# Wide DMA transposes, odd K heads through GpSimd's queue, and x kept by tiles, in a statically ordered two-layer attention and feed-forward kernel

## The chip, the cores and the metric

One core of one Trainium2 chip. The metric is device time in microseconds (us), lower is better. The six executions of the kernel before agree within 0.3%. Each run also lists the mean clock that TensorE was granted, as a share of full speed; it was between 0.97 and 1.00. The engines are TensorE (PE for its matmuls, PEld for its weight loads), VectorE (DVE), ScalarE (ACT), GpSimd (POOL) and the sync engine (SP), which here only issues DMAs.

## The reference

The input x has 2048 tokens of 512 values in bf16. Two times in turn: a memory-augmented attention, then a gated feed-forward layer, each on a layer-normalised x and with a residual sum.

```python
def reference(A_x, ...):
    x = A_x
    x = x + _A_ref(_layernorm(x), wq, wk, wv, wo, beta)   # 32 heads of 16, 4 segments of 512 tokens
    x = x + _B_ref(_layernorm(x), w1, w3, w2)             # silu(x w1) * (x w3), then w2; width 1376
    ... both once more ...

# _A_ref, for each segment s of 512 tokens and each head:
    p = softmax(q k^T * scale + causal mask);  a_dot = p v
    a_mem = (phi(q) M) / (phi(q) z + 1e-6)     # M, z: what earlier segments left
    o = g * a_mem + (1 - g) * a_dot            # then o @ wo
    M += phi(k)^T v;  z += sum(phi(k))
```

## The kernel before

The program lists its operations with what each reads and writes. A scheduler inside it then fixes, before anything runs, the order of instructions on every engine and the semaphore waits. It has a model of durations, and two tables (PRIO and GATE) that shift single groups of operations; the tables look fitted by search. At run time each engine goes through its list in this order, and what stands behind a waiting instruction starts later too: in the profile before, TensorE stood up to 1.7 us ahead of the memory update.

There are eight passes: two layers of four segments. Logits use four strips of the tensor array at a time (the four matmuls of a set start within 10 ns of each other, the median for 256 columns in the trace before). K of the odd heads is moved to other partitions, into `km`. Where data must be turned (tokens to columns or back), a DMA transpose of 128 x 512 elements does it, issued by the sync engine; only the x of the first two attention passes is turned on TensorE.

```python
xn_r = ring("xn", 4, [P, D])          # normalised x, one tile of 128 tokens each
xs_r = ring("xs", 4, [P, 512])        # attention outputs out of PSUM
xg_r = ring("xg", 3, [P, LT, 2, P])   # the same, turned

# normalise a tile, then turn it: one DMA a tile
S.add([o_dve(512, False, 1.45)], lambda e, ...: e.tensor_scalar(
    xn_r[xn.slot][:], x_tok[:, tt, :], mean, rstd, op0=ALU.subtract, op1=ALU.mult), ..., name="norm")
dmaT(lambda e, ...: e.dma_start_transpose(dt_[dst.slot][:, :, i * 128:(i + 1) * 128], xn_r[xn.slot][:, :]), ..., name="xT")
# (first two attention passes: four transposes on TensorE, line 628, instead of the DMA)

# odd heads of K, from the third pass on: 4 copies of 64 KB on the sync queue
S.add([("sp", 450.0, 2200.0)], lambda e, r=r: e.dma_start(km_r[z.km.slot][r], k_r[z.k.slot][r]), dmaq="sp", ..., name="km")

# memory update: pk turned by four DMAs, then 32 matmuls of 136 columns (line 735)
for G in range(NCG):
    dmaT(lambda e, G=G: e.dma_start_transpose(pkt_r[kt.slot][:, G, :, :], pk_r[pkb.slot][:, G, :]), ..., name="pkT")

# causal mask on the diagonal blocks, on GpSimd, after exp on ScalarE
pool(lambda e, ...: e.affine_select(e_r[ebuf.slot][:, :, c:c + 128], ..., fill=0.0), 512, ..., name="mask")

# attention output: two PSUM banks, two copies out, two DMAs
for X, xs, es in XS:
    ev(lambda xs=xs: xs_r[xs.slot][:], lambda X=X: bank(X), 512, ..., name="evX")
    dmaT(lambda e, ...: e.dma_start_transpose(dst(), xs_r[xs.slot][:]), ..., name="XT")
```

In the views below, line numbers of the kernel before and (in brackets) of the changed one are: projections of q and k 676 (677), of v 671 (672), logits 844 (852), probabilities times values 895 (903), memory update 735 (738), output projection 963 (952), gate and up 994 (983), down 1022 (1011), transposes of x on TensorE 628 (628), normalisation 618 (618), mask 866 (874). Of the names, `xn` is normalised x, `xs` attention outputs out of PSUM (TensorE's output memory, `psall`), `xg` the same turned, `og` the outputs made ready for the last projection, `e` the exponentials, `pk` phi(k). `W` is a set of buffers that many share: `W<-xn` turns x, `W<-W` turns pk, `W<-og` turns the outputs for the last projection.

Of the kernel before, what the change touches and what calls it, by code (L numbers as in the profile page):

```python
# [8 lines left out]
P = 128  # L9
# [16 lines left out]
LAT = 100.0  # L26
LAT_SAME = 50.0
DMA_SLACK = 500.0
# [4 lines left out]
SLACK = {"pe": 60.0, "act": 90.0, "dve": 60.0, "pool": 0.0, "sp": 300.0}  # L33
LOOK = {"pe": 90.0, "act": 90.0, "dve": 10.0, "pool": 10.0, "sp": 40.0}
C_AGE = 1200.0
MARGIN = {"rd": 200.0}
# [331 lines left out]
def o_pe(ns):  # L368
# [7 lines left out]
    ("", 0): 20, ("bnst", 3): -2.3, ("bnst", 7): -0.15, ("dacc", 4): -4, ("evX", 0): 1000.2, ("evk", 1): 1400,  # L376
    ("evk", 5): 1005, ("evq", 0): 300, ("evq", 7): 1751.7, ("evv", 0): 99.8, ("g", 3): -20, ("g", 5): 301.3,
    ("gp", 4): 998, ("hm", 6): 84.9, ("k", 4): -0.35, ("k", 5): 20.3, ("k", 7): -250, ("km", 2): -0.3,
    ("km", 4): 1000, ("ldwk", 0): -1.3, ("mblk", 2): 300, ("mrec", 3): -300, ("ph", 6): -0.6, ("phmin", 0): -100,
    ("phmin", 2): 0.05, ("q", 1): -300, ("q", 2): 0.6, ("q", 3): -550.05, ("q", 4): -0.3, ("q", 6): -999.7,  # L380
    ("rd", 0): 300, ("rdg", 1): -1, ("t", 7): -20, ("tanh", 5): -0.75, ("u", 1): -500, ("u", 4): -2002, ("u", 6): 780,
    ("v", 5): -0.15,
}
GATE = {
    ("bnst", 2): -1, ("bnst", 3): 1, ("bnst", 6): 3, ("ph", 0): -22, ("phexp", 0): -15, ("v", 1): -30, ("v", 6): 8,
    ("v", 7): 6,
# [3 lines left out]
def build(nc, A_x, A_wq, A_wk, A_wv, A_wo, A_beta, B_w1, B_w3, B_w2, out):  # L390
# [25 lines left out]
    xn_r = ring("xn", 4, [P, D])  # L416
# [7 lines left out]
    xs_r = ring("xs", 4, [P, 512])  # L424
    xg_r = ring("xg", 3, [P, LT, 2, P])
# [47 lines left out]
    def dmaT(fn, q="sp", **k):  # L473
        return S.add([(q, 1290.0, 2500.0)], fn, dmaq=q, mode="T", **k)
# [31 lines left out]
    if WARM:  # L506
        dve(lambda e: e.memset(xs_r[0][:], 0.0), 200, writes=["warm"], prio=CP - 1)

        def spin(e, B=new("B")):
            for _ in range(2):  # L510
                o = e.matmul(bank(B), xs_r[0][:, 0:128], xs_r[0][:], start=True, stop=True)
            return o
        wb = spin.__defaults__[0]
        pools["xs"].prev[0] = [pe(spin, 2 * MM512 * (2 if i < 4 else 1), reads=["warm"], writes=[(wb, 0)], bufs=[wb], prio=1e4, name="warm")
                               for i in range(WARM)]
# [14 lines left out]
    HEAD = (("sp", "q"), ("act", "3"), ("sp", "2"), ("act", "k"))  # L530
# [66 lines left out]
    def layer_norm(s, name, prio, gates=(), fine=False, turn=False, part=(0, LT), dst=None):  # L597
# [17 lines left out]
        for i in tiles:  # L615
            tt = 4 * s + i
            xn = new("xn")
            S.add([o_dve(512, False, 1.45)], lambda e, i=i, tt=tt, xn=xn: e.tensor_scalar(  # L618
                xn_r[xn.slot][:], x_tok[:, tt, :], ln_r[st.slot][:, i, 6:7], ln_r[st.slot][:, i, 9:10],
                op0=ALU.subtract, op1=ALU.mult), reads=[("x", tt), (st, 3, i), (st, 1, i)], writes=[(xn, 0)],  # L620
                bufs=[st, xn], hold=[dst], prio=prio, name="norm")
            if turn:
                B = new("B")
                tb = lambda B=B: bank(B).bitcast(BF16)[:, 0:512].rearrange("p (g c) -> p g c", g=NCG)

                def flip(e, xn=xn, tb=tb):
                    for cg in range(NCG):
                        o = e.transpose(tb()[:, cg, :], xn_r[xn.slot][:, 128 * cg:128 * cg + 128], ident[:])
                    return o
                pe(flip, 4 * 62, reads=[(xn, 0), "ident"], writes=[(B, 0)], bufs=[B, xn], prio=-900, name="xt")  # L630
                ev(lambda i=i: dt_[dst.slot][:, :, i * 128:(i + 1) * 128], tb, 512, reads=[(B, 0)], writes=[(dst, i)],
                   bufs=[B, dst], prio=-900, name="evt")
                continue
            dmaT(lambda e, i=i, xn=xn: e.dma_start_transpose(dt_[dst.slot][:, :, i * 128:(i + 1) * 128], xn_r[xn.slot][:, :]),
                 reads=[(xn, 0)], writes=[(dst, i)], bufs=[xn, dst], prio=prio, name="xT")
# [14 lines left out]
    def project(s, g, X, first):  # L650
        z = Seg()
        z.q, z.k, z.km, z.va = new("W"), new("W"), new("km"), new("va")
        if first:
            jobs = []
            for hf in range(2):
                for A in (0, 2):
                    jobs += [("q", (A, A + 1), hf), ("k", (A, A + 1), hf)]
# [3 lines left out]
        for n, (kind, Gs, hf) in enumerate(jobs):  # L661
# [5 lines left out]
            for a, G in enumerate(Gs):  # L667
                for cg in range(NCG):
                    st, sp_ = cg == 0, cg == NCG - 1
                    if kind == "v":  # L670
                        fn = lambda e, cg=cg, G=G, B=B, st=st, sp_=sp_: e.matmul(  # L671
                            bank(B), xa_r[X.slot][:, cg, 128 * G:128 * G + 128], wv_sb[:, cg, :], start=st, stop=sp_)
                        rd = [(X, G)]
                    else:
                        w = wq_sb if kind == "q" else wk_sb
                        fn = lambda e, cg=cg, G=G, B=B, st=st, sp_=sp_, w=w, a=a, W=W, c0=c0: e.matmul(  # L676
                            bank(B)[:, W * a:W * a + W], w[:, cg, 128 * G:128 * G + 128], xa_r[X.slot][:, cg, c0:c0 + W],
# [20 lines left out]
            elif kind == "k" and Gs[0] == NCG - 1:  # L698
                for pg in range(4):
                    r = slice(32 * pg + 16, 32 * pg + 32)  # L700
                    S.add([("sp", 450.0, 2200.0)], lambda e, r=r: e.dma_start(km_r[z.km.slot][r], k_r[z.k.slot][r]), dmaq="sp",
                          mode="T", reads=[(z.k, a, h) for a in range(NCG) for h in range(2)], writes=[(z.km, pg, "p")],
# [18 lines left out]
    def memory_update(g, z, pkb):  # L721
        kt = new("W")
        for G in range(NCG):
            dmaT(lambda e, G=G: e.dma_start_transpose(pkt_r[kt.slot][:, G, :, :], pk_r[pkb.slot][:, G, :]),
                 reads=[(pkb, G // 2)], writes=[(kt, G)], bufs=[pkb, kt], prio=g + 0.1, name="pkT")
        mb = new("mb")
        for hf in range(2):
# [10 lines left out]
            pe(fn, 8 * 65, reads=[(kt, 2 * hf), (kt, 2 * hf + 1)] + [(z.va, i) for i in range(LT)], writes=[(B, 0)],  # L738
# [49 lines left out]
    def unit_list(part):  # L788
# [9 lines left out]
        else:  # L798
            for G in (0, 2):
                out.append(([(A, ee, t1 - 1) for A in (G, G + 1) for ee in range(2)], []))  # L800
# [12 lines left out]
    JOIN = True  # L813
    HP = -1e6
# [6 lines left out]
    def attention(s, g, z, oms, parts):  # L821
        z.ot = new("W")
        cnt = 0
        for pi, part in enumerate(parts):
# [4 lines left out]
            for ui, (blocks, done, N) in enumerate(todo):  # L829
# [3 lines left out]
                for pgs in groups:  # L833
# [14 lines left out]
                    u = pe(lg, N / 2.4 + 20, mode="R", reads=[(z.k, b[0], b[2] // 2) for b in blocks] +  # L848
# [30 lines left out]
    def attend(s, g, z, pr, part, G, ees, where, xg, gates):  # L879
        t0, t1 = part  # L880
        W = 128 * (t1 - t0)
        both = W == 512 and len(ees) == 2
        sets = [(ee,) for ee in ees] if both else [ees]
        XS = [(new("B"), new("xs"), es) for es in sets]
        keys = [(G, ee, j) for ee in ees for j in range(t1)]
        spot = {ee: (X, W * es.index(ee)) for X, xs, es in XS for ee in es}

        def av(e):
# [11 lines left out]
        pe(av, ncol / 2.4 + 10 * len(keys), mode="C", reads=[t for k in keys for t in where[k][3]] + [(z.va, j) for j in range(t1)],  # L900
           writes=[(X, 0) for X, xs, es in XS], bufs=[X for X, xs, es in XS] + [z.va] + list(ebs.values()),
           hold=[xs for X, xs, es in XS], prio=pr, gates=gates, name="C%d.%d" % (G, ees[0]))
        for X, xs, es in XS:
            ev(lambda xs=xs: xs_r[xs.slot][:], lambda X=X: bank(X), 512, reads=[(X, 0)], writes=[(xs, 0)], bufs=[X, xs],
               prio=g - 100.2, name="evX")
            if len(es) == 1:
                dst = lambda es=es: xg_r[xg.slot][:, :, es[0], :]
            else:
                dst = lambda: xg_r[xg.slot][:].rearrange("p t e c -> p (t e) c")[:, 0:4, :]
            dmaT(lambda e, dst=dst, xs=xs: e.dma_start_transpose(dst(), xs_r[xs.slot][:]), reads=[(xs, 0)],  # L910
                 writes=[(xg, ee) for ee in es], bufs=[xs, xg], prio=pr, name="XT")

    def normalise(g, z, part, G, xg, oms):
# [8 lines left out]
        sums = lambda: xg_r[xg.slot][:].rearrange("p t e (a c) -> p (t e a) c", c=32)[:, 0:n, 16]  # L922
        gv = lambda: gg[:, 1, 8 * G:8 * G + 8].rearrange("p (a e) -> p e a", e=2)

        def scaled(e):
            a, b = rd_r[rd.slot][:, 0, 0:n], rd_r[rd.slot][:, 1, 0:n]
            if full:
                v = "p (t e a) -> p t e a"
                w = gv()[:, None, :, :].to_broadcast([P, nt, 2, 4])
            else:  # L930
                v = "p (e t a) -> p e t a"
                w = gv()[:, :, None, :].to_broadcast([P, 2, nt, 4])
            return e.tensor_tensor(b.rearrange(v, e=2, a=4), a.rearrange(v, e=2, a=4), w, ALU.mult)
        dve(lambda e: e.reciprocal(rd_r[rd.slot][:, 0, 0:n], sums()), 7.2 * n, reads=[(xg, 0), (xg, 1)], writes=[(rd, 0)],
            bufs=[xg, rd], prio=pr, name="rd")
        dve(scaled, n + 90, reads=[(rd, 0), "g1"], writes=[(rd, 1)], bufs=[rd], prio=pr, name="rdg")
        ogv = lambda: og_r[og.slot][:].rearrange("p t (a e d) -> p t a e d", e=2, d=DH)
        for k in range(2):
            def fn(e, k=k):
                if full:  # L940
                    src = xg_r[xg.slot][:, :, k, :].rearrange("p t (a c) -> p t a c", c=32)[:, :, :, 0:16]
                    r = rd_r[rd.slot][:, 1, 0:n].rearrange("p (t e a) -> p t e a", e=2, a=4)[:, :, k, :]
                    return e.tensor_tensor(ogv()[:, :, :, k, :], src, r[:, :, :, None].to_broadcast([P, nt, 4, DH]), ALU.mult)
                src = xg_r[xg.slot][:].rearrange("p t e c -> p (t e) c")[:, 2 * k:2 * k + 2, :]
                r = rd_r[rd.slot][:, 1, 4 * nt * k:4 * nt * k + 4 * nt].rearrange("p (t a) -> p t a", a=4)
                return e.tensor_tensor(ogv()[:, 0:nt, :, k, :], src.rearrange("p t (a c) -> p t a c", c=32)[:, :, :, 0:16],
# [163 lines left out]
```

## Time and profile before

| | before |
|---|---|
| time, median of 6 runs | 500.5 us (499.94 to 501.57) |
| span of the profiled run | 498.1 us |
| TensorE busy, idle by the profile | 480.9 us, 17.2 us |
| VectorE, ScalarE, GpSimd busy | 403.4, 394.3, 235.9 us |
| sync queue in DMA issues | 259 us |
| DMA transposes | 180 |

TensorE is busy all but 17 us. These are the issues that the change touches, with the median time from issue to landing in the last column:

```profile
km<-W SPq DMA_DIRECT2D x24, 64.0 KB, 2.4
...
xg<-xs SPq DMA_TRANSPOSE x64, 2.4
...
W<-xn SPq DMA_TRANSPOSE x56, 2.5
```

### The profile page before, as it was taken

The numbers are of one execution on the slowest core, as the hardware profiler recorded it, in microseconds if no ns is written. First come the engines' busy times: TensorE is split into PE (matmuls) and PEld (weight loads), VectorE is DVE, ScalarE is ACT, GpSimd is POOL, SyncE is SP. The second block draws the span as 40 slices with busy tenths as digits, with TensorE's granted clock in tenths as the row PEclk, the third lists the DMA queues.
The fourth block names the chain that finished last, engine by engine and source line by source line (L and its number), as shares of the span: only waits on it lengthen the run. The fifth ranks groups of instructions, "written<-read, shape, count | busy, mean of one in ns | idle before, by whom it ended". The sixth has DMA issues, their size and how long they took to land.

```text
span 498.1 us, 10481 instructions
## 1 busy us (share of the span) xinstructions
PE 480.9 (97%) x4198; PEld 214.9 (43%) x4198; DVE 403.4 (81%) x802; ACT 394.3 (79%) x350; POOL 235.9 (47%) x350
## 2 busy tenths in 40 slices
PE   7999898999999999999999999999999999999997
PEld 4443335654444344344444344444344334444443
DVE  5899998997888689889967889889984797479572
ACT  3999898899989997799988999788987898731230
POOL 4857444575455555645544436445645563610000
PEclk9999999999999999999999999999999999999999
DMA  6956834422232241341441303522322222220201
GB/s 198 313 89 128 137 74 96 67 59 48 54 68 52 64 70 38 76 86 22 68 93 43 75 22 75 95 45 54 71 49 54 53 43 54 65 53 12 74 1 42
DMA packets 104160, 35.86 MB, mean 72 GB/s; under 512 B 96976, under 2 KB 102096, under 8 KB 104112
## 3 DMA queue, kind: packets, MB, share of 16 engines
q1 hardware_dynamic: 102432, 31.94, 31.1%
q0 software_dynamic: 720, 2.46, 1.8%
q10 hardware_dynamic: 960, 0.79, 0.6%
q8 instruction: 33, 0.54, 0.5%
q14 instruction: 15, 0.12, 0.1%
HBM read 8.43 MB, written 2.10 MB: 21 GB/s over the span
## 4 chain that ended last, share of the span: by engine, by line
PE 74%; DVE 16%; DMA 4%; ACT 3%; issue 1%; SPq 1%; POOL 0%
PE psall L994 29%; PE psall L1022 15%; PE psall L844 8%; PE psall L676 7%; PE psall L895 5%; PE psall L963 3%; PE psall L671 3%; DVE ln L605 2%; ACT e L853 2%; DVE xn L618 2%; DVE W L481 2%; DVE x_tok L967 2%; DVE W L713 1%; DVE xs L481 1%; DMA W<-W 1%; DVE W L715 1%
## 5 line engine op out<-in xcount | busy, mean ns | idle before, releaser
L853 ACT ACTIVATE e<-psall 128x2048 bf16<-128x2048 f32 (+1 forms) x180 | 301.0, 1702 | 37.9 <-PE psall L844 36.0
L866 POOL TENSOR_SCALAR_AFFINE_SELECT e<-e 128x512 bf16<-128x512 bf16 x256 | 163.5, 658 | 165.4 <-ACT e L853 164.0
L994 PE MATMUL psall<-W,w 128*128 128x512 bf16 (+3 forms) x792 | 169.6, 356 | 0.5 <-DVE h L1011 0.2
L994 PEld LDWEIGHTS psall<-W,w 128*128 128x128 bf16 (+1 forms) x792 | 73.6, 100 | 75.0 <-issue 12.0
L1022 PE MATMUL psall<-w,h 128*128 128x512 bf16 (+1 forms) x352 | 85.7, 380 | 0.0
L1005 ACT ACTIVATE th<-psall 128x512 bf16<-128x512 f32 (+2 forms) x89 | 51.9, 593 | 40.8 <-PE psall L994 40.5
L1007 DVE SCALAR_TENSOR_TENSOR gp<-th,psall 128x512 bf16<-128x512 bf16 (+2 forms) x89 | 59.2, 673 | 15.4 <-ACT th L1005 14.8
L1011 DVE SCALAR_TENSOR_TENSOR h<-gp,psall 128x512 bf16<-128x512 bf16 (+1 forms) x89 | 59.4, 673 | 8.9 <-PE psall L994 8.5
L1022 PEld LDWEIGHTS psall<-w,h 128*128 128x128 bf16 (+1 forms) x352 | 32.0, 98 | 37.6 <-issue 5.3
L605 DVE BATCH_NORM_STATS2 ln<-x_tok 128x6 f32<-128x512 bf16 x64 | 42.6, 680 | 2.1 <-DMA x_tok<-in_A_x_dram 1.6
L1027 DVE TENSOR_TENSOR x_tok<-psall,x_tok 128x512 bf16<-128x512 f32 x32 | 22.1, 689 | 26.8 <-PE psall L1022 26.8
L895 PE MATMUL psall<-e,va 128*32 128x256 bf16 (+3 forms) x1088 | 41.4, 293 | 1.0 <-DVE h L1011 0.4
L844 PE MATMUL psall<-W,km 32*128 32x256 bf16 (+3 forms) x544 | 40.8, 291 | 1.0 <-ACT e L853 1.0
L844 PE MATMUL psall<-W 16*128 16x256 bf16 (+3 forms) x544 | 41.3, 294 | 0.5 <-ACT e L853 0.4
L481 DVE CAST xs<-psall 128x512 bf16<-128x512 f32 x40 | 27.0, 685 | 14.0 <-PE psall L895 13.9
L676 PE MATMUL psall<-W,wk 128*128 128x512 bf16 (+1 forms) x144 | 34.8, 357 | 2.1 <-DVE xs L481 1.0
L676 PE MATMUL psall<-W,wq 128*128 128x512 bf16 (+1 forms) x144 | 34.8, 357 | 0.9 <-ACT W L480 0.9
L618 DVE TENSOR_SCALAR xn<-x_tok,ln 128x512 bf16<-128x512 bf16 x64 | 33.5, 567 | 2.2 <-POOL ln L612 2.1
L481 DVE CAST W<-psall 128x512 bf16<-128x512 f32 x45 | 30.3, 680 | 4.4 <-PE psall L676 4.1
L671 PE MATMUL psall<-wv,W 128*128 128x512 bf16 x128 | 33.8, 381 | 0.0
L895 PEld LDWEIGHTS psall<-e,va 128*32 128x32 bf16 x1088 | 24.0, 96 | 19.5 <-issue 3.5
L844 PEld LDWEIGHTS psall<-W 16*128 16x128 bf16 x544 | 13.1, 91 | 43.5 <-ACT e L853 37.0
(66 smaller groups left out, 441.2 us busy)
## 6 DMA issues: line engine op xcount, KB each, us to landing
w<-in_B_w_dram SPq DMA_DIRECT2D x4, 688.0 KB, 8.9
out_dram<-x_tok SPq DMA_DIRECT2D x16, 128.0 KB, 1.8
km<-W SPq DMA_DIRECT2D x24, 64.0 KB, 2.4
w<-in_B_w_dram POOLq DMA_DIRECT2D x3, 384.0 KB, 3.7
xg<-xs SPq DMA_TRANSPOSE x64, 2.4
x_tok<-in_A_x_dram POOLq DMA_DIRECT2D x2, 512.0 KB, 6.4
W<-xn SPq DMA_TRANSPOSE x56, 2.5
W<-og SPq DMA_TRANSPOSE x36, 2.4
```

The lines of the kernel that those rows point to most:

```text
L481: return e.tensor_copy(dst(), src())
L605: dve(lambda e, i=i, tt=tt: e.bn_stats(ln_r[st.slot][:, i, 0:6], x_tok[:, tt, :]), 540, reads=[("x", tt)], writes=[(st, 0, i)], bufs=[st], ...
L676: fn = lambda e, cg=cg, G=G, B=B, st=st, sp_=sp_, w=w, a=a, W=W, c0=c0: e.matmul(bank(B)[:, W * a:W * a + W], w[:, cg, 128 * G:128 * G + 1 ...
L844: o = e.matmul(S4[:, sps(pg), c:c + n], kk[32 * pg:32 * pg + r, G, 128 * j:128 * j + 128], q_r[z.q.slot][32 * pg:32 * pg + r, G, 128 * t1 ...
L853: act(lambda e, N=N, ebuf=ebuf, pgs=pgs, sps=sps: e.activation(e_r[ebuf.slot][:, pgs[0]:pgs[-1] + 1, 0:N], S4[:, sps(pgs[0]):sps(pgs[-1]) ...
L866: pool(lambda e, ebuf=ebuf, c=c: e.affine_select(e_r[ebuf.slot][:, :, c:c + 128], e_r[ebuf.slot][:, :, c:c + 128], pattern=[[0, 4], [1, 128]],
L895: o = e.matmul(bank(X)[32 * pg:32 * pg + 32, base + W - n:base + W], va_r[z.va.slot][:, j, h:h + 32], e_r[eb.slot][:, pg, c:c + n], start= ...
L994: prev = pe(lambda e, i=i, cg=cg, ft=ft, B=B, w=w: e.matmul(bank(B)[0:width(ft), W * i:W * i + W], w[:, cg, 128 * ft:128 * ft + width(ft)] ...
L1005: act(lambda e, fw=fw, NW=NW, B=B, th=th: e.activation(th_r[th.slot][0:fw, 0:NW], bank(B)[0:fw, 0:NW], ACT.Tanh, scale=0.5), NW, reads=[(B ...
L1007: dve(lambda e, fw=fw, NW=NW, B=B, th=th, gp=gp: e.scalar_tensor_tensor(gp_r[gp.slot][0:fw, 0:NW], th_r[th.slot][0:fw, 0:NW], 1.0, bank(B) ...
L1011: dve(lambda e, fw=fw, NW=NW, B=B, gp=gps[fg], h=hs[fg]: e.scalar_tensor_tensor(h_r[h.slot][0:fw, 0:NW], gp_r[gp.slot][0:fw, 0:NW], 0.5, b ...
L1022: prev = pe(lambda e, ft=ft, fw=fw, B=B, h=h, c=c: e.matmul(bank(B), h_r[h.slot][0:fw, c:c + 128], w2_sb[0:fw, ft, :], start=(ft == 0), st ...
```

## The change

Its intent: fewer, larger DMA transposes, so that the sync queue has time and pairs land sooner; x by tiles (tile, then column), because a transpose of two tiles writes them so; the small copies of odd K heads off that queue; and an order fitted anew. The scheduler's constants and tables are all new.

```diff
-LAT = 100.0 ; LAT_SAME = 50.0 ; DMA_SLACK = 500.0            (three lines, joined here)
+LAT = 80.0 ; LAT_SAME = 30.0 ; DMA_SLACK = 1200.0
-MARGIN = {"rd": 200.0}
+MARGIN = {"XT": 800.0, "km": 2000.0, "mde": 1200.0, "oT": 2000.0, "stx": 3000.0, "xT": 2000.0, ...}
 ... SLACK, LOOK and both tables PRIO and GATE: all values new ...
-    xn_r = ring("xn", 4, [P, D])
+    xn_r = ring("xn", 2, [P, 2, D])
-    xs_r = ring("xs", 4, [P, 512])
-    xg_r = ring("xg", 3, [P, LT, 2, P])
+    xs_r = ring("xs", 3, [P, 2, 512])
+    xg_r = ring("xg", 3, [P, 2 * LT, P])
-    HEAD = (("sp", "q"), ("act", "3"), ("sp", "2"), ("act", "k"))
+    HEAD = (("sp", "k"), ("act", "3"), ("sp", "2"), ("act", "q"))
 ... normalised x, two tiles by one DMA:
-            dmaT(lambda e, i=i, xn=xn: e.dma_start_transpose(dt_[dst.slot][:, :, i * 128:(i + 1) * 128], xn_r[xn.slot][:, :]),
-                 reads=[(xn, 0)], writes=[(dst, i)], bufs=[xn, dst], prio=prio, name="xT")
+            elif k == 1:
+                dmaT(lambda e, i=i, xn=xn: e.dma_start_transpose(
+                    dt_[dst.slot][:, i - 1:i + 1, :].rearrange("p i (g c) -> p (i g) c", c=P), xn_r[xn.slot][:].rearrange("p i d -> p (i d)")),
+                     reads=[(xn, 0), (xn, 1)], writes=[(dst, i - 1), (dst, i)], bufs=[xn, dst], prio=prio, name="xT")
 ... the first segment:
-                    jobs += [("q", (A, A + 1), hf), ("k", (A, A + 1), hf)]
+                    jobs += [("k", (A, A + 1), hf), ("q", (A, A + 1), hf)]
 ... odd K heads:
-                    S.add([("sp", 450.0, 2200.0)], ... dmaq="sp", mode="T", ...
+                    S.add([("pool", 1000.0, 2000.0)], ... dmaq="pool", size=65536, ...
 ... pk, four DMAs become two:
-        for G in range(NCG):
-            dmaT(lambda e, G=G: e.dma_start_transpose(pkt_r[kt.slot][:, G, :, :], pk_r[pkb.slot][:, G, :]),
+        for hf in range(2):
+            dmaT(lambda e, hf=hf: e.dma_start_transpose(
+                pkt_r[kt.slot][:, 2 * hf:2 * hf + 2, :, :].rearrange("p g i c -> p (g i) c"),
+                pk_r[pkb.slot][:, 2 * hf:2 * hf + 2, :].rearrange("p g n -> p (g n)")),
 ... attention outputs, one DMA for both banks:
-            dmaT(lambda e, dst=dst, xs=xs: e.dma_start_transpose(dst(), xs_r[xs.slot][:]), reads=[(xs, 0)],
+        dmaT(lambda e: e.dma_start_transpose(xg_r[xg.slot][:, 0:n, :], xs_r[xs.slot][:].rearrange("p a n -> p (a n)")[:, 0:128 * n]),
 ... readers of x, for example gate and up:
-                        xf_r[X.slot][:, cg, 128 * t0:128 * t1], start=(cg == 0), stop=(cg == NCG - 1)),
+                        xf_r[X.slot][:, t0:t1, 128 * cg:128 * cg + 128], start=(cg == 0), stop=(cg == NCG - 1)),
```

A list of attention units behind a flag that is off, other assumed times of matmuls (smaller) and of wide transposes in the scheduler's model, and the same arithmetic of the softmax sums on the new layout are left out here.

## The prediction

> **What bounds the kernel now.** I read the page's busy times first, then the stretches of the span, then the waits, then the timeline where the longest waits lie.
>
> ```profile
> PE 480.9 (97%) x4198; PEld 214.9 (43%) x4198; DVE 403.4 (81%) x802; ACT 394.3 (79%) x350; POOL 235.9 (47%) x350
> ...
> PEclk9999999999999999999999999999999999999999
> ...
> PE 74%; DVE 16%; DMA 4%; ACT 3%; issue 1%; SPq 1%; POOL 0%
> ```
>
> TensorE is busy for 97% at full clock and makes up 74% of the chain that ended last; DMA is 4% of that chain. So TensorE sets the time. How much of its 480.9 us is real work? In the last stretch nothing but feed-forward matmuls runs, and 88 of 512 columns start in 19.00 us, 216 ns each, which is 512 columns at 2.4 per ns (213 ns) and 3 ns. I added the columns of all matmuls at that rate (the attention matmuls of lines 844 and 895 run four at a time on strips of the array, so I divide theirs by four): feed-forward 150 + 75, projections 55 + 27 + 27, logits 34, values 34, memory and transposes 12, warm-up 3: 418 us. From the first matmul's start to the last one's is 493 us, so 75 us lie between the matmul starts as loss. Most of that is structural: each of the 176 groups of logits costs 170 ns beyond its columns, about 30 us in all[...], and other groups some 0.1 us each. The columns and the groups are the same in the changed kernel. What a schedule can change is the rest. Taking the steady 2.5 to 3 us of loss in 25 us (it is 2.6 us from 275 to 300 us) as the floor, the excess is about 20 us: 1.5 us before 25 us, 7.5 us from 25 to 50, 6 us from 50 to 75, 2 us from 75 to 100, and about 0.5 us in each later 25 us.
>
> ```profile
> 20.00:30.00 10.00, 9.28 (x122) 4.49 (x120) 9.48 (x16) 9.80 (x12) 9.54 (x14) 1.00 0.97 175
> ...
> 50.00:60.00 10.00, 8.35 (x121) 4.02 (x121) 9.48 (x23) 8.73 (x10) 3.43 (x7) 1.00 0.85 142
> ...
> 80.00:100.00 20.00, 17.19 (x217) 12.70 (x216) 17.77 (x37) 16.91 (x16) 10.02 (x15) 1.00 0.46 79
> ...
> 440.00:498.00 58.00, 54.58 (x253) 24.80 (x251) 37.56 (x67) 10.74 (x18) 2.79 (x3) 1.00 0.12 32
> ```
>
> The columns are the stretch, its length, and the busy time of PE, PEld, DVE, ACT and POOL, then clock and DMA. TensorE has visible holes in 50 to 60 and 80 to 100 us, and in the last stretch, where 3.4 us are missing: that is the tail, last sum and store, which stays. The stretch from 20 to 60 us is the first segment's attention, when VectorE and ScalarE are both at 95% or so and no feed-forward work exists yet to fill in.
>
> ```profile
> PEld psall L735 <- DMA W<-W: 3.7, 4, 1.9
> ...
> PE psall L735 <- DMA W<-W: 2.7, 2, 1.7
> ...
> PEld psall L676 <- DMA W<-xn: 1.1, 1, 1.1
> ...
> PEld psall L994 <- DMA W<-xn: 1.0, 2, 0.6
> ```
>
> These are the waits of TensorE for transposes: total us, times, longest. Line 735 is the memory update and needs pk transposed by four DMAs of 128 KB. The gaps between starts before line 735 are 1.9 us at 92.7, 1.2 at 102.7, 0.6 at 195.6 and 0.5 at 330.9; less a normal change of 0.1 each, about 3.8 us. With 1.2 us at 62 (a projection waits for its normalised x) and some 1 us before line 994, transposes cost TensorE about 6 us. The timeline shows why:
>
> ```profile
> 87.72 2.65 SPq L724 DMA_TRANSPOSE W<-W  x2
> ...
> 90.41 1.71 SPq L955 DMA_TRANSPOSE W<-og  x1
> ...
> 92.16 2.57 SPq L910 DMA_TRANSPOSE xg<-xs  x2
> ...
> 93.21 0.67 PE L735 MATMUL psall<-va,W 128*128 128x136 bf16 x8 [0.98 <-DMA W<-W]
> ```
>
> From 87.7 to 94.7 us the sync queue does nothing but issue transposes, one after another, and the memory update stands behind the second of its pair.
>
> [...]97% busy, 43% weight loads, and 418 of 498 us (84%) by my count of columns. [...]Here the 64 KB copies land in 2.4 us and the 128 KB transposes in 2.4 to 2.5 us[...]: twice the width should not double the time. [...]The trace has only seven such issues, 541 to 958 ns each, against 589 ns (median) for the copies on the sync queue; [...]the normalisation of one tile takes 319 ns at best, 412 in the median and 1307 at most.
>
> **The change part by part.**
> - Wide transposes. Per-pass transposes of attention outputs go from 64 to 36 (28 wide, and the first segment's 8 stay narrow), of normalised x from 56 to 28 wide, of pk from 24 to 12 wide; the 36 of the outputs for the last projection stay: 180 become 112. Issue on the sync queue took 231 us in all, 1.29 us each. With 44 narrow at 1.26 us and 68 wide at 1.4 us (an estimate: the program's own constant goes from 1290 to 1400 ns for a wide one) it takes about 150 us. The trace cannot show whether a wide one is that cheap.
> - Latency. A pair of pk now lands 1.25 + 2.5 = 3.75 us after the first issue; one wide one about 3.0 us (the diff's constant, an estimate again). All four after 6.3 us at best, then 4.4 us. For x, four tiles are normalised in 4 x 0.57 us; the wide one has to wait for two of them, so I expect 1 us less there, not 2. For attention outputs the two copies out of PSUM run on two engines side by side, and the wide one waits for both: no gain.
> - Odd K copies on GpSimd. 24 x 0.66 = 16 us leave the sync queue, and 24 x about 0.76 us (the median of the w issues) = 18 us come onto GpSimd, 236 to 254 us, 51% of the span. They need no TensorE time and are wanted only by the next segment, so 0 us, unless they hold up masks: a mask is used two units later, some 5 us, so a delay of 0.8 us fits in.
> - x tile by tile. The moving operand becomes four runs of 128 columns instead of one of 512. The memory update already streams runs of 17 out of 24 columns: 136 columns take a mean of 226 ns including the modelled tail, against 223 for a transposing or memory matmul of 128. So 0 us.
> - Buffers. Attention outputs get three slots for a pair each instead of two pairs; normalised x has the same room in pairs, which come free later. About even.
> - Order. All constants of the static scheduler are new: larger assumed DMA delay (500 to 1200 ns), margins for operations that tended to come late, and in the first segment k before q, so that the odd K copies can start a little earlier.
>
> Sum: of the 6 us of transpose waits I take 4 us as gained; of the other 14 us of excess, most of it in the first segment bound by three engines at once, I give the new order 3 us; I charge 1 us for busier GpSimd and for coarser pairs. Net 6 us: 500.7 - 6 = 494.7.
>
> **The rivals.**
> First, hidden anyway: the sync queue is busy only 52% of the span (259 of 498 us), its DMA waits on TensorE are a few us, and TensorE has other work in order. Then only the 1 us at a few places is won and the new order is noise: 498 to 501. For it speaks the 74% of TensorE in the chain; against it the visible holes before line 735.
> Second, the order is worth more: if the new constants fill the first 75 us, 15 of the 20 us of excess could go[...]: 486 to 489. Against it: ScalarE is at 9.8 of 10 us from 20 to 30, and the list of attention units is the same.
> Third, a new wait: GpSimd's masks stand behind a DMA issue that waits for k[...]. Each of 24 issues costing TensorE 0.3 us would be 7 us and eat all of it: 500 to 504. GpSimd at 47% speaks against it.
>
> **Range and chances.** The middle case gives 495; the first rival is the upper end, the second the lower: 488 to 501. Faster by over 2% means under 490.7, which needs 10 of the 20 us of excess: 0.21. Slower by over 2%, over 510.7, needs something that no row shows: 0.02. Within 2%: 0.77.
>
> **What would show it right or wrong.** In the profile after: 112 transposes, wide ones of about 1.4 us of issue and about 3 us to landing; waits of line 735 for DMA under 2 us in total; matmuls of lines 994 and 676 still starting every 216 ns; GpSimd near 254 us; TensorE busy still 475 to 482 us with a span shorter by the holes at 50 to 60 and 80 to 100 us. I am wrong if wide transposes take twice as long, if matmuls on the tile-wise x start more slowly, if masks wait behind GpSimd's DMA issues, or if the loss from 25 to 75 us falls by more than half.

The forecast's sum: 4 us of waits gained, 3 us by the order, 1 us charged, so 500.7 - 6 = 494.7 us. The second rival stands on its 15 us (500.7 - 15 = 485.7), the third on masks behind a DMA issue. That a wide transpose would not take twice as long was the estimate, from the 2.4 and 2.5 us to landing. "Such issues" are DMAs issued from GpSimd. The rate of 2.4 columns per ns is the trace's own: matmuls of 256 columns start 109 ns apart and those of 512 columns 216 ns (medians), so 256 columns more take 107 ns. The 170 ns of a group of logits are counted from its first start to the next other matmul's, 29.9 us over the 176 groups.

## The result and the profile after

The changed kernel takes 493.64 us (median of 6 runs, 491.25 to 496.19) against 500.5. The ratio is 0.9865, with a 95% interval of 0.9833 to 0.9897: within 2%, and clear of noise. Ratios here are the mean time of one kernel's runs over that of the other's of the same rounds, so not quite the ratio of the medians quoted.

The page of the changed kernel, the lines that answer to the first fence of the prediction:

```profile
PE 481.1 (98%) x4198; PEld 216.6 (44%) x4198; DVE 402.2 (82%) x803; ACT 390.8 (79%) x344; POOL 250.8 (51%) x379
...
PEclk9989999999999999999999999999999999999999
...
PE 81%; DVE 14%; DMA 2%; ACT 1%; POOL 1%; issue 0%
```

TensorE has the same busy time in a span of 491.6 us: its idle time fell from 17.2 to 10.5 us, and those 6.7 us are the gain (6.5 us between the two spans). DMA is now 2% of the chain instead of 4%. One thing is new: the third digit of the clock is 8. Before the last matmul, the records of the clock have one stretch at half speed in the changed kernel, from 29.0 to 32.4 us, and none in the kernel before.

The same stretches as in the prediction (columns: length, PE, PEld, DVE, ACT, POOL, clock, DMA share, GB/s):

```profile
20.00:30.00 10.00, 8.69 (x131) 4.68 (x129) 9.16 (x18) 10.00 (x12) 9.06 (x14) 0.95 0.79 105
50.00:60.00 10.00, 9.03 (x123) 4.18 (x121) 9.93 (x23) 9.47 (x11) 6.21 (x11) 1.00 0.85 165
80.00:100.00 20.00, 20.00 (x229) 13.72 (x229) 19.35 (x42) 18.66 (x17) 13.29 (x19) 1.00 0.34 68
440.00:491.00 51.00, 48.33 (x224) 22.08 (x222) 32.49 (x57) 8.94 (x15) 2.17 (x2) 1.00 0.13 34
```

The hole of 2.8 us from 80 to 100 us is gone, that from 50 to 60 us is smaller by 0.7 us, and from 20 to 30 us one has opened (9.28 busy before, 8.69 now). The tail is as it was.

TensorE's waits: the first line, for a normalised x, is new in size (1.2 us before); the second is all that is left of its own waiting for pk.

```profile
PE psall L628 <- DVE xn L618: 2.1, 2, 1.3
...
PE psall L738 <- DMA W<-W: 0.7, 1, 0.7
```

And the DMA issues (count, size where known, median us to landing):

```profile
km<-W POOLq DMA_DIRECT2D x24, 64.0 KB, 2.9
...
xg<-xs SPq DMA_TRANSPOSE x36, 2.8
W<-og SPq DMA_TRANSPOSE x36, 2.4
...
W<-xn SPq DMA_TRANSPOSE x28, 3.2
...
W<-W SPq DMA_TRANSPOSE x12, 3.3
```

There are 112 transposes instead of 180. A wide one takes 1.41 us of the sync queue on average (the 40 of x and pk, 56.5 us) and lands in 3.2 to 3.3 us (the median of attention outputs, 2.8, mixes 28 wide and 8 narrow ones). The queue's issues add up to 158 us.

I counted the loss between matmul starts again, as in the prediction, now by the kind of work that starts late (both traces hold all 4198 matmuls):

| loss ahead of | before, us | after, us |
|---|---|---|
| memory update | 5.2 | 1.7 |
| projections of q and k | 12.1 | 9.8 |
| memory reads | 2.8 | 1.0 |
| probabilities times values | 5.8 | 4.9 |
| logits | 24.0 | 23.6 |
| gate, up, down | 14.1 | 14.1 |
| v, output projection, transposes on TensorE | 10.7 | 13.3 |
| all | 74.7 | 68.4 |

### The profile page after: what moved, and what is told of

It is laid out like the page before. It is cut to its first block, busy times and chain, and to the rows that moved or that the text cites. A ratio compares the mean times of both kernels' runs of the same rounds, so it can differ in the third digit from the quotient of the medians.

```text
span 491.6 us, 10384 instructions
## 1 busy us (share of the span) xinstructions
PE 481.1 (98%) x4198; PEld 216.6 (44%) x4198; DVE 402.2 (82%) x803; ACT 390.8 (79%) x344; POOL 250.8 (51%) x379
## 4 chain that ended last, share of the span: by engine, by line
PE 81%; DVE 14%; DMA 2%; ACT 1%; POOL 1%; issue 0%
PE psall L983 31%; PE psall L1011 15%; PE psall L852 10%; PE psall L677 8%; PE psall L903 7%; PE psall L952 5%; PE psall L672 4%; DVE W L480 2%; DVE xn L618 2%; DMA W<-W 1%; DVE ln L604 1%; DVE W L716 1%; PE psall L738 1%; DVE xs L480 1%; PE psall L778 1%; ACT e L861 1%
## 5 line engine op out<-in xcount | busy, mean ns | idle before, releaser
L983 PE MATMUL psall<-W,w 128*128 128x512 bf16 (+2 forms) x792 | 172.6, 357 | 0.2 <-DVE gp L996 0.2
L994 ACT ACTIVATE th<-psall 128x512 bf16<-128x512 f32 (+1 forms) x89 | 51.2, 594 | 35.0 <-PE psall L983 34.9
L996 DVE SCALAR_TENSOR_TENSOR gp<-th,psall 128x512 bf16<-128x512 bf16 (+1 forms) x89 | 58.8, 673 | 19.4 <-ACT th L994 18.7
L480 DVE CAST W<-psall 128x512 bf16<-128x512 f32 x51 | 34.1, 681 | 5.0 <-PE psall L677 4.6
L936 POOL TENSOR_TENSOR og<-xg,rd 128x256 bf16<-128x256 bf16 (+1 forms) x40 | 26.6, 672 | 20.6 <-DVE rd L930 14.0
L672 PE MATMUL psall<-wv,W 128*128 128x512 bf16 x128 | 35.4, 388 | 0.0
L677 PE MATMUL psall<-W,wq 128*128 128x512 bf16 (+1 forms) x144 | 33.1, 357 | 0.3 <-issue 0.3
```

What stands on the lines that cost most here:

```text
L480: return e.tensor_copy(dst(), src())
L672: fn = lambda e, cg=cg, G=G, B=B, st=st, sp_=sp_: e.matmul(bank(B), xa_r[X.slot][:, G, 128 * cg:128 * cg + 128], wv_sb[:, cg, :], start=st ...
L677: fn = lambda e, cg=cg, G=G, B=B, st=st, sp_=sp_, w=w, a=a, W=W, c0=c0: e.matmul(bank(B)[:, W * a:W * a + W], w[:, cg, 128 * G:128 * G + 1 ...
L983: prev = pe(lambda e, i=i, cg=cg, ft=ft, B=B, w=w: e.matmul(bank(B)[0:width(ft), W * i:W * i + W], w[:, cg, 128 * ft:128 * ft + width(ft)] ...
L994: act(lambda e, fw=fw, NW=NW, B=B, th=th: e.activation(th_r[th.slot][0:fw, 0:NW], bank(B)[0:fw, 0:NW], ACT.Tanh, scale=0.5), NW, reads=[(B ...
L996: dve(lambda e, fw=fw, NW=NW, B=B, th=th, gp=gp: e.scalar_tensor_tensor(gp_r[gp.slot][0:fw, 0:NW], th_r[th.slot][0:fw, 0:NW], 1.0, bank(B) ...
```

## The experiments

My theory after reading the traces had three parts. First, the wide transposes take away waits of the memory update and of projections, about 4 us. Second, the new order is fitted to them and gives some more. Third, about 2 us are lost again around 27 us by a normalisation that VectorE could not finish. The rivals: the order does it all and the width is idle; or the move of the K copies matters.

To try one part, I mostly kept the issue order of the changed kernel on every engine exactly as it is and changed what an instruction does in its place. A new run of the scheduler on a changed program would give another order, and, as the runs show, that alone moves the time by tens of us.

### Wide transposes issued as two narrow ones, in place

```diff
-                dmaT(lambda e, i=i, xn=xn: e.dma_start_transpose(
-                    dt_[dst.slot][:, i - 1:i + 1, :].rearrange(...), xn_r[xn.slot][:].rearrange("p i d -> p (i d)")),
+                dmaT(lambda e, i=i, xn=xn: [e.dma_start_transpose(
+                    dt_[dst.slot][:, i - 1 + a, :].rearrange("p (g c) -> p g c", c=P), xn_r[xn.slot][:, a, :]) for a in range(2)], nd=2,
 ... the same for pk and for attention outputs; nd DMAs add 16 * nd to their semaphore ...
```

> The changed kernel with every instruction in the same place, but each wide transpose issued as two narrow ones back to back (68 wide become 136 narrow; completion counted over both). If the wide transposes carry the gain by themselves, the sync queue goes from 158 us back to about 235 us, the second half lands 0.6 us or more later, and waits of the memory update for its transposes come back: 495.5 to 498 us. If the gain is in the order and its slack, 493 to 494.5 us, as the changed kernel (493.6).

Measured: 521.37 us (519.05 to 522.99), ratio to before 1.0402 (1.0366 to 1.0437). That is 27 us over the changed kernel (the difference of the ratios, 0.0537, times 500.5 us, and the same way below), six times the most that I expected, and 20 us over the kernel before, which uses narrow ones throughout. TensorE's waits in its profile (here line 986 is gate and up, 1014 down, 741 the memory update, 681 q and k):

```profile
PE psall L986 <- DMA W<-xn: 4.6, 3, 2.2
PE psall L1014 <- DVE h L1003: 3.8, 1, 3.8
PE psall L741 <- DMA W<-W: 3.3, 2, 2.7
PE psall L681 <- DMA W<-xn: 2.8, 1, 2.8
```

Waits for transposes on TensorE come to 11.4 us (the three lines with DMA and 0.7 at the output projection), against 0.9 us in the changed kernel. VectorE waits 17.8 us for attention outputs, against 0.8. The clock falls to half three times, for 3.4 us each (the run's mean is 0.990): twice after a wait for a transpose (2.65 and 2.82 us), once after the 3.8 us for VectorE's h. So the new order leans on the wide transposes: it has no room for 1.25 us more of issue at these places. It does not show that the width is worth 27 us, as the kernel before lives with narrow ones at 500 us in an order made for them.

### Which kind of transpose the order leans on

The same edit on one kind alone.

> As narrow_in_place, but only the 28 wide transposes of normalised x are issued as two narrow ones each. There TensorE stood 7.4 us for these transposes, and its clock fell. If these are what the order leans on, 500 to 510 us; if the loss was shared by all three kinds, about a third of 28 us: 499 to 504; if the queue's total load made it, 494 to 497 us.

Measured: 506.97 us (503.07 to 509.21), ratio 1.0095 (1.0037 to 1.0153): 11.5 us over the changed kernel.

> As narrow_in_place, but only the 12 wide transposes of pk before the memory update. By the prediction this is where the wide ones gain (about 4 us): 496 to 499 us. If the new order gives the memory update enough slack, 493 to 495 us.

Measured: 498.32 us (493.78 to 499.99), ratio 0.9919 (0.9868 to 0.9970): 2.7 us over, but the intervals overlap.

> As narrow_in_place, but only the 28 wide transposes of attention outputs. VectorE stood 17.8 us for these there, TensorE not directly. By the prediction no gain from them: 493 to 496 us. If the late outputs hold up VectorE and the sync queue behind it, 499 to 512 us.

Measured: 497.74 us (494.29 to 499.96), ratio 0.9916 (0.9868 to 0.9964): 2.6 us over, and the intervals overlap too.

The three come to 17 us, not 27, so the losses feed on each other; that they do so through the queue that all share is likely, but not shown. Most of it is in the transposes of x, which TensorE waits for with a whole feed-forward pass or projection behind them. I had put the main gain at pk. The profile of narrow_x shows 2.9 us of TensorE waiting for x directly, and 10.2 us at half clock (a mean of 0.990). In the pk and attention runs the one execution at full clock took 493.78 and 494.29 us; the others had a clock of 0.989 to 0.996. So part of what was lost in those two goes with the clock. Whether all of it does, single executions can't tell: the changed kernel's only one at full clock took 491.25 us, in another session. Whether the narrow issues set off these drops is not shown either. In the profile with narrow pk (clock 0.993) they start at 9.4 and 33.3 us, in that with narrow attention outputs (0.993) at 8.7 us; but the first pk is turned at 25 us, and the attention outputs of the first segment are narrow in any case. The drops at 9 us cannot come from the edit. The one at 33.3 us follows a normalisation of 2.89 us, which the changed kernel has without the edit (below).

### The odd K copies back on the sync queue, in place

```diff
+        for op in issue:
+            if op.name == "km" and op.dmaq == "pool":
+                op.eng = op.dmaq = "sp"
 ... the lists of both engines and the semaphores are then made anew from the same order ...
```

> The changed kernel in the same order, but the 24 copies of odd K heads are issued by the sync queue at their places instead of by GpSimd. GpSimd loses 24 x 0.52 us of issues. If their move matters, because GpSimd's masks or VectorE wait less or because the sync queue is blocked at the waits for k, the time changes by over 2 us; I expect it not to matter: 492.5 to 495 us, GpSimd busy 238 us instead of 251.

Measured: 492.79 us (492.38 to 493.87), ratio 0.9842 (0.9801 to 0.9883); the changed kernel's is 0.9865. No difference that can be told. GpSimd is busy 240 us instead of 251. The move to GpSimd's queue neither helps nor harms.

### One mask waits for one normalisation

In the timeline of the changed kernel, GpSimd has six masks in a row, and VectorE a normalisation of one tile in that time:

```profile
25.50 3.58 POOL L874 TENSOR_SCALAR_AFFINE_SELECT e<-e 128x512 bf16<-128x512 bf16 x6
...
26.33 2.90 DVE L618 TENSOR_SCALAR xn<-x_tok,ln 128x512 bf16<-128x512 bf16 x1
...
29.28 0.61 PE L628 MATMUL psall<-ident,xn 128*128 128x128 bf16 x4 [1.28 <-DVE xn L618]
```

The normalisation, 0.41 us as a median, takes 2.90 us and ends 0.15 us after the row of masks. The next transpose on TensorE needs it, and 1.28 us of TensorE go. The same normalisation takes 2.90 us in the profile of narrow_in_place too. To break the row without taking any wait away, I added one:

```diff
+        norm = [op for op in issue if op.group == ("norm", 1)][0]
+        mask = [op for op in issue[issue.index(norm):] if op.eng == "pool"][0]
+        mask.deps[norm.seq] = norm
```

> The changed kernel with one dependency added: the next mask on GpSimd after the first normalisation of the second segment waits for that normalisation (which took 2.90 us behind six masks in a row in the profile, then TensorE stood 1.28 us and its clock fell to half for 3.4 us). If that row of masks holds VectorE up, the normalisation takes 0.4 to 1.1 us, the clock stays at 1.00, and the time is 490 to 491.5 us in nearly all runs. If the long normalisation or the clock has another cause, the clock still falls (0.993 to 0.997) and the time stays at 493 to 494.5 us.

Measured: 491.8 us (five runs from 491.15 to 491.86 at a clock of 0.999 or 1.000, one of 495.64 at 0.992), ratio 0.9826 (0.9790 to 0.9861). Against the changed kernel that is 2.0 us less, and the intervals overlap. The one execution of the changed kernel at full clock took 491.25 us, no more than these five, so the gain is in how often the clock drops: in five of six executions there, in one of six here. The profile shows each step:

```profile
25.70 1.22 POOL L878 TENSOR_SCALAR_AFFINE_SELECT e<-e 128x512 bf16<-128x512 bf16 x2
...
26.53 0.54 DVE L622 TENSOR_SCALAR xn<-x_tok,ln 128x512 bf16<-128x512 bf16 x1
...
27.14 2.64 POOL L878 TENSOR_SCALAR_AFFINE_SELECT e<-e 128x512 bf16<-128x512 bf16 x4 [0.22 <-DVE xn L622]
...
27.35 1.36 DVE L622 TENSOR_SCALAR xn<-x_tok,ln 128x512 bf16<-128x512 bf16 x2
```

The normalisation takes 0.54 us, at a cost of 0.22 us of GpSimd. So the row of masks did hold it up. Not every row does so to its end: here two more normalisations take 0.72 us each within the row of four and end 0.14 to 0.15 us after the mask under way, and two in the kernel before, at 27.7 and 28.4 us, take as long (0.72 and 0.71 us) and end 0.15 us after theirs. Why the one at 26.33 us was held for all of the row stays open. What the edit does to the clock is seen in two stretches, first of the changed kernel, then of this one (PE busy is the second number after the length, the clock the third from the end):

```profile
25.60:29.00 3.40, 2.40 (x32) 0.83 (x31) 3.40 (x3) 3.40 (x5) 3.40 (x6) 1.00 1.32 164
29.00:32.40 3.40, 3.12 (x16) 1.44 (x17) 3.30 (x11) 2.08 (x3) 0.07 (x1) 0.50 0.73 77
```

```profile
25.60:29.00 3.40, 3.25 (x41) 1.22 (x40) 3.40 (x8) 3.40 (x5) 3.18 (x6) 1.00 1.19 174
29.00:32.40 3.40, 3.24 (x26) 1.20 (x25) 2.67 (x8) 3.40 (x5) 0.79 (x2) 1.00 0.72 78
```

After a stretch with TensorE busy 2.40 of 3.40 us (71%), and no gap in it longer than 1.28 us, the next 3.4 us run at half clock, 16 matmuls in place of 26. After 3.25 us busy they don't.

The busy share alone does not decide it, though: in the kernel before, TensorE is busy for 2.11 us of the 3.4 us from 48.7 us (62%), and the clock stays at 1.00 there and in the 3.4 us after. What separates the two is not shown; no experiment set how much work such a stretch holds.

### q before k in the first segment

```diff
-    HEAD = (("sp", "k"), ("act", "3"), ("sp", "2"), ("act", "q"))
+    HEAD = (("sp", "q"), ("act", "3"), ("sp", "2"), ("act", "k"))
-                    jobs += [("k", (A, A + 1), hf), ("q", (A, A + 1), hf)]
+                    jobs += [("q", (A, A + 1), hf), ("k", (A, A + 1), hf)]
```

> The changed kernel with q before k in the first segment, loads and projections, as in the kernel before; all else, constants too, as changed, so the static order may shift in later places. If k first is what makes the first 30 us denser or what sets off the clock drop, the clock goes to 1.00 and the time changes by 1.5 us or more; I expect a later start of the odd K copies by some 0.3 us and a time of 492 to 496 us, mostly by a shifted order.

Measured: 511.99 us (510.86 to 513.02), ratio 1.0219 (1.0181 to 1.0257), 18 us over the changed kernel. The first 30 us cannot hold that: the scheduler made another order throughout, with tables that no longer fit, and the clock (0.980 to 0.987) is lower too. As a trial of k first it is of no use. It serves as a measure of how much an unfitted order costs.

### Structure and order crossed

Four kernels: each structure with the other's constants, and both structures with the two tables emptied and the remaining constants of before. The assumed times of matmuls and transposes stay with their structure.

```diff
-PRIO = { ... }
-GATE = { ... }
+PRIO = {}
+GATE = {}
```

> The changed structure (wide transposes, copies on GpSimd, x by tiles, k first) with all scheduler constants of the kernel before. If the structure carries the gain, 494 to 499 us. If the constants are fitted to one structure and the gain is theirs, as the 512 us of q_first suggests, 503 to 518 us.

> The structure of before with all scheduler constants of the changed kernel. If the constants carry the gain on their own (more slack for DMA), 493 to 498 us. If they are fitted to the wide transposes, 503 to 520 us.

> The kernel before with the two tables of per-operation priorities and gates emptied, other constants as before. A fitted order lost: 508 to 525 us. It is the base for the next run.

> The changed structure with the same emptied tables and the other constants of before. If the wide transposes help by themselves, in an order fitted to neither, it is 3 to 8 us below old_untuned; if only the fitting matters, within 3 us of it or above.

Measured, medians in us, with the ratio to before:

| | tables emptied | constants of before | constants of after |
|---|---|---|---|
| old structure | 524.73 (1.0489) | 500.5 | 514.94 (1.0284) |
| new structure | 515.16 (1.0306) | 515.31 (1.0303) | 493.64 (0.9865) |

The intervals of the four new ones, in reading order: 1.0465 to 1.0512, 1.0251 to 1.0318, 1.0267 to 1.0344, 1.0234 to 1.0372. Neither part carries the gain alone: each structure with the other's constants is some 15 us slower than the kernel before. Fitting is worth 24 us to the old structure (524.7 to 500.5) and 21.5 us to the new one (515.2 to 493.6, where the other constants change too). With both tables emptied, the new structure is 9.6 us faster, a little more than I had put down; with both fitted, 6.9 us.

Why 9.6? The waits of TensorE for transposes are 2.0 us in the unfitted old one and 0.2 in the unfitted new one; the sync queue's issues take 259 and 154 us; and the clock is at half for 30.7 us in the profile of the old one (mean 0.970) and 10.2 us in the new one's (0.990). By the recorded share of one half, the 20 us more cost at most 10 us of work (an estimate from these numbers), so the clock could be most of the difference; how much of it the narrow transposes caused stays open.

### The two that were not slower, together

> mask_waits_norm and km_on_sp together: the normalisation is not held up by the row of masks, and GpSimd issues no copies. If both gains hold (2 us, and 0 to 1 us): 490.5 to 491.8 us, clock 0.999 or more. If copies on the sync queue cost slack there: 492 to 494 us.

This is mask_waits_norm with the K copies on the sync queue. Measured: 491.69 us (490.48 to 493.33), ratio 0.9801 (0.9768 to 0.9833), the lowest of all, 3.2 us below the changed kernel by the ratios. Its interval and that of mask_waits_norm alone overlap, so the second edit is not shown to add anything. In its profile (clock 0.999) the clock does not drop before the last matmul. It beats the kernel before by 2.0%.

## Why the prediction was right

The time, 493.64 us, is 1.1 us from the 494.7 us forecast, and most steps to it were of the forecast size. That it came so near is in part luck: the changed kernel's own executions span 4.9 us, next to nothing was won where 3 us were forecast, and the 1 us charged stood for something else. By its steps:

- **Bound by TensorE, structural loss fixed.** Right. Matmul count and busy time are the same; the loss ahead of logits is 23.6 us against 24.0.
- **4 of 6 us of transpose waits gained.** About right in size, and at the place named: the loss ahead of the memory update fell by 3.5 us, of 3.8 us of excess. The other 2.3 us at q and k I had not split off. That the width took these waits away, and not the order, is not shown: narrow_pk lost 2.7 us, with overlapping intervals. What I had not seen is that the new order leans most on the transposes of x (11.5 us in narrow_x against 2.7 in narrow_pk). Three slips of mine belong here. The sum starts from 500.7 us, where the median is 500.5. The times of gaps and the loss by 25 us in the prediction are on the trace's own clock, 10.9 us ahead of the profile's, in which the four gaps before line 735 lie at 83.7, 93.2, 186.8 and 320.7 us. And the 1.2 us "at 62 us" are a projection that starts at 50.8 us after a wait for attention outputs to leave PSUM; the wait for x is at 63.3 us and costs 0.8 us of starts. The sum of 6 us becomes 5.6.
- **Wide transposes of about 1.4 us and 3 us to landing.** Right: 1.41 us as a mean (1.31 as a median), and 3.2 to 3.3 us.
- **K copies worth 0 us.** Right, by km_on_sp. The cost on GpSimd was over-estimated: 0.50 us each (median), not 0.76; GpSimd came to 250.8 us, not 254.
- **x by tiles worth 0 us.** Right: a run of 88 gate and up matmuls of 512 columns still starts every 216 ns (25 of them take 5.56 us with the tail of the last).
- **3 us from the new order, in the first segment.** The place was wrong, and the amount cannot be told from that of the wide transposes. Up to 75 us the loss is 24.6 us against 25.1, so next to nothing was won where I looked for it (the half clock at 29 us lies in that stretch and may hide up to 2 us). From 75 to 125 us it fell from 9.2 to 7.2 us, which holds most of the memory update's gain, and from 125 to 200 us from 10.6 to 8.5 us.
- **1 us charged for GpSimd and buffers.** Something of that size was lost, but by another way: six masks in a row held up one normalisation, TensorE stood for 1.28 us, and the clock then fell for 3.4 us. That is 2.0 us by mask_waits_norm, with overlapping intervals. The third rival had GpSimd's issues of the K copies hold up others, but the first of those is issued at 74 us, 48 us later.
- **The rivals.** The first (hidden anyway) fell with the loss at the memory update. The second (the order is worth more, 486 to 489 us) fell with the time, and with the loss up to 75 us, which it had falling by 15. That the order brings nothing without the structure is seen in old_struct_new_order, at 514.9 us. But the prediction took width and order as separate terms of a sum. The runs show that they are not: crossed, they make 15 us worse, so the 4 and the 3 us have no meaning apart from each other. The sum may have held because both kernels were fitted to their own structure, so that only the waits still visible in the trace counted; this is not shown.

What stays open is how the 6.9 us divide between width and order, and how much of the crossed and unfitted results is the clock. k before q in the first segment was not tried by itself, as q_first changed the whole order.

## What to carry to other kernels

Where a static order is fitted to durations, a change of structure without a new fit tells little: here the changed structure took 515.3 us with the old constants and 493.6 with its own, and the 22 us between them are over two times what the structure brought (6.9 to 9.6 us). To learn what one part does, keep the order and change the instruction in its place, and then read a loss as what the order leans on, not as what the part is worth. And look for short waits that come in a thin stretch of TensorE: one instruction of VectorE behind a row of GpSimd instructions stopped TensorE for 1.28 us, and half clock followed; without it the median is some 2 us lower.
